# Two layers of cached attention and gated MLP on one core: weights through a ring of four equal places, block transposes between up and down, values that give up quarters

## The chip, the core and the metric

The kernel runs on one core of one Trainium2 chip. The time is device microseconds of one execution; smaller is better. Three runs of the kernel before took 2713.55, 2713.64 and 2716.07 us (median 2713.64 us). One further execution was profiled; it took 2714.15 us, of which 2712.4 us are the span from its first to its last instruction.

## What is computed

Two batch rows (B = 2) of width 576 pass twice through the same attention block and the same gated MLP:

```python
x = x + attention(layernorm(x))       # wq, K cache, V cache, wo
x = x + mlp(layernorm(x))             # (gelu(h @ w_gate) * (h @ w_up)) @ w_down
x = x + attention(layernorm(x))       # same weights, same caches
x = x + mlp(layernorm(x))
```

The caches hold 32 heads of 8192 positions by 128 floats for each batch row, in float32: one head of one batch row is 4.19 MB of keys and as much of values. The weights are wq 576x4096, wo 4096x576, w_gate and w_up 576x4608, and w_down 4608x576.

## The kernel before, in words

**Work.** There are 64 pairs of a head and a batch row, numbered n in the loop of `attention` (line 524). For each n the keys are multiplied by the query in four quarters (`multiply`, lines 401 to 417: VectorE multiplies 128x2048 elements, GpSimd adds the upper half of each head vector to the lower), `add_up` (line 419) reduces each quarter to scores on VectorE, `peak`, `highest` and `softmax` (lines 434 to 453) find the maximum and the exponentials through TensorE, VectorE and ScalarE, and `values` (line 463) multiplies them with the values: 16 matrix products on TensorE. The work of n-1 after its last quarter is interleaved by hand with the quarters of n (lines 524 to 553): this order is fixed in the program, engine by engine.

**Memory.** One tile `space` (line 102) of 50176 floats a partition holds all that is streamed in. It has five slots of 8192 floats, each for the keys or the values of one pair, and behind them, from RING = 40960 on, a sixth slot with 1024 floats more. In the MLP of layer 0 and at the start of attention 1 the weights pass only through the part behind RING, since the five slots before it hold what attention 1 will use first: the keys of the last two pairs and the values of the last three are kept from layer 0 (`keys_held`, `values_held`, line 223), and attention 1 walks the pairs backward (line 281).

**Order of the loads.** All loads are issued by the queue of SyncE, in one order: `plan_attention` and `plan_mlp` (lines 230 to 278) append them to a list, and `pump` (line 117) issues from its head as long as `Arena` finds free room; `done` (line 124) frees room and pumps again. A load waits for the last instruction that read or wrote what lay in its room, and everything behind it in the queue waits with it.

**Weights in layer 0's MLP.** w_gate and w_up come in nine pieces each of 2304 floats a partition (`ONE`, line 173); w_down comes in thirds of 1728 floats, the last of them split into 1152 and 576 (`thirds`, lines 217 to 219). Each is put where `Arena.ring` (line 74) finds room first. wq of attention 1 comes in nine pieces of 2048 floats, each to one of four fixed addresses (line 236).

**Start of attention 1.** The keys of pair 2 (counted in the backward walk) come in quarters to the room that wq left; those of pair 3 come in quarters to the room of pair 0's keys, those of pair 4 to that of pair 1's keys (line 245), each quarter as soon as `add_up` is done with the quarter that lay there. The values of pair 3 come next, whole, when all 16 products of `values(0)` are done (lines 477 to 481), then the keys of pair 5, whole, after `values(1)`.

**Between up and down.** `mlp` (line 575) scales the products of gate and up (`o`, lines 591 and 592), turns them to the layout that w_down needs by 18 small products on TensorE with a selection matrix `spread` (lines 595 to 601), copies the gate half out of PSUM, computes the GELU on VectorE and ScalarE (lines 605 to 610), writes `hT` (line 612) and multiplies with w_down (line 620).

Of the kernel before, what the change touches and what calls it, by code (L numbers as in the profile page):

```python
# [15 lines left out]
P = 128  # L16
# [15 lines left out]
EG = DF // 8  # L32
HG = EG // 2
# [7 lines left out]
END = NSLOT * SLOT + 1024  # L41
RING = 5 * SLOT
HELD = 5


class Arena:


    def __init__(self):
        self.live = {}  # L50
        self.freed = [0] * (NSLOT + 1)
        self.clock = 0
        self.at = RING

    def clear(self, lo, n):
        return all(hi <= lo or l >= lo + n for l, hi in self.live.values())

    def slot(self, key, allowed):

        for s in sorted(allowed, key=lambda s: self.freed[s]):  # L60
            if self.clear(s * SLOT, SLOT):
                for k in range(4):
                    self.quarter(key, s * SLOT, k)
                return s * SLOT
        return None

    def quarter(self, key, at, k):
        lo = at + k * PART
        if not self.clear(lo, PART):
            return False  # L70
        self.live[key, k] = (lo, lo + PART)
        return True
# [18 lines left out]
def decode_layers(ctx, tc, x_in, kc, vc, wq, wo, wg, wu, wd, out):  # L91
# [23 lines left out]
    queue, ready, slots = [], {}, {}  # L115

    def pump():
        while queue:
            t = queue[0][1]()
            if t is None:  # L120
                return
            ready[queue.pop(0)[0]] = t
# [5 lines left out]
    def cache(key, src, hb, allowed, pieces=1, where=None):  # L128

        rows = src[hb % B, hb // B].rearrange("(p j) d -> p j d", p=P)  # L130

        def load(at, lo, hi):
            t = space[:, at:at + SLOT].rearrange("p (j d) -> p j d", d=DH)
            nc.sync.dma_start(t[:, lo:hi, :], rows[:, lo:hi, :])
            return t

        def make():
            at = arena.slot(key, allowed)
            if at is None:
                return None  # L140
            slots[key] = at
            for lo in range(0, J, J // pieces):
                t = load(at, lo, lo + J // pieces)
            return t

        def make_quarter(k):
            at = slots[key] = RING if where == "ring" else slots[where]
            return load(at, k * JC, (k + 1) * JC) if arena.quarter(key, at, k) else None

        if where is None:  # L150
            queue.append((key, make))
        else:

            for k in ((NU + i) % 4 if where == "ring" else i for i in range(4)):
                queue.append((key, lambda k=k: make_quarter(k)))

    def eighths(key, w, us, width, lo, hi=None):

        n = 4 * len(us)

        def make():
            at = arena.ring(key, n * width, lo, hi)
            if at is None:
                return None
            t = space[:, at:at + n * width].rearrange("p (c w) -> p c w", c=n)
            src = w.rearrange("r (e w) -> (r e) w", w=width).rearrange("(p j) w -> p j w", p=P)
            nc.sync.dma_start(t, src[:, 4 * us[0]:4 * us[0] + n, :])
            return t

        queue.append((key, make))  # L170


    ONE = [range(u, u + 1) for u in range(NU)]
    THREE = [range(u, u + 3) for u in range(0, NU, 3)]
    PIECES = {
        ("wq", 0): THREE, ("wq", 1): ONE, ("g", 0): ONE, ("u", 0): ONE, ("g", 1): THREE, ("u", 1): THREE[:-1] + ONE[-3:],
    }

    def down(key, t0, lo, hi, first):

        def make():
            at = arena.ring(key, (hi - lo) * D, first)
            if at is None:
                return None
# [478 lines left out]
```

## Time and profile before

| what | value |
|---|---|
| median of the runs | 2713.64 us |
| profiled execution | 2714.15 us |
| its span | 2712.4 us |
| VectorE busy | 1887.3 us, 70% of the span |
| GpSimd busy | 1209.4 us, 45% |
| TensorE matmul busy | 1144.8 us, 42% |
| ScalarE busy | 82.6 us, 3% |
| packets of the SyncE queue, as a share of 16 DMA engines' span | 99.4% |

In the page the span is cut into 40 slices of 67.8 us; a digit is the busy share in tenths, and a row gives the GB/s in each slice. A row of a window table has the window, its length, the busy time of each engine with its instruction count, the granted TensorE clock, the mean busy share of the 16 DMA engines, and GB/s. A row of the chain of waits has the start, the length and the name of what the end waited for; "DMA tile<-source" there runs from a transfer's issue to its landing. A row of the timeline has start, length, engine, line, operation, tiles, shapes and count, and in brackets the idle time before it with what ended it; "SPq" is SyncE's queue issuing a transfer.

### The profile page before, as it was taken

What the parts mean: (1) busy time and instruction counts of PE and PEld (TensorE: products, weight loads), DVE (VectorE), ACT (ScalarE), POOL (GpSimd) and SP (SyncE); (2) the same over time, 40 slices, a digit from 0 to 9 for tenths busy, and PEclk for the clock granted to TensorE, in tenths of its full rate; (3) what the DMA queues carried; (4) which work ended last, traced back from release to release, by engine and by line L of the source; (5) the groups of instructions that cost most, each with busy time, mean ns of one, the idle gap of its engine ahead of it and who ended that gap; (6) DMA issues with size and microseconds to landing.
All of it is one profiled execution on the core that took longest, in us unless ns stands there. A gap on an engine that the chain in (4) does not pass through costs nothing.

```text
span 2712.4 us, 19378 instructions
## 1 busy us (share of the span) xinstructions
PE 1144.8 (42%) x7392; PEld 406.0 (15%) x7392; DVE 1887.3 (70%) x1809; ACT 82.6 (3%) x391; POOL 1209.4 (45%) x522
## 2 busy tenths in 40 slices
PE   2344434343434343444555434343434343434356
PEld 0111111111111111111211111111111111111122
DVE  5777777777777777776039877777777777777740
ACT  0000000000000000000000000000000000000000
POOL 3545454444445454443016554444444454445420
PEclk7666666666666666666757766666666666566667
DMA  9999999999999999999999999999999999999998
GB/s 418 432 433 431 431 430 431 432 432 431 430 432 432 431 431 431 431 432 414 404 358 409 430 431 432 432 431 430 431 431 432 431 430 431 432 431 431 432 426 378
DMA packets 49099, 1155.48 MB, mean 426 GB/s; under 512 B 5464, under 2 KB 5488, under 8 KB 7664
## 3 DMA queue, kind: packets, MB, share of 16 engines
q1 hardware_dynamic: 48968, 1154.24, 99.4%
q8 instruction: 58, 0.95, 0.1%
q14 instruction: 33, 0.27, 0.0%
q10 hardware_dynamic: 40, 0.01, 0.0%
HBM read 1154.23 MB, written 0.00 MB: 426 GB/s over the span
## 4 chain that ended last, share of the span: by engine, by line
DMA 80%; DVE 10%; PE 8%; issue 2%; POOL 0%; ACT 0%; DVEq 0%; POOLq 0%; SPq 0%; ACTq 0%
DMA space<-in_A_k_cache_dram 45%; DMA space<-in_A_v_cache_dram 28%; PE acc L472 7%; DVE space L413 5%; DVE S L422 3%; DMA space<-in_B_w_down_dram 2%; DMA space<-in_B_w_gate_dram 2%; DMA space<-in_A_wo_dram 1%; DMA space<-in_B_w_up_dram 1%; DMA space<-in_A_wq_dram 1%; DVE osb L489 1%; PE xps L620 0%; PE acc L584 0%; PE acc L377 0%; POOL space L417 0%
## 5 line engine op out<-in xcount | busy, mean ns | idle before, releaser
L417 POOL TENSOR_TENSOR space<-space 128x1024 f32<-128x1024 f32 x512 | 1206.4, 2356 | 1257.1 <-DVE space L413 1221.7
L413 DVE TENSOR_TENSOR space<-space,qp 128x2048 f32<-128x2048 f32 x512 | 1164.7, 2275 | 483.8 <-DMA space<-in_A_k_cache_dram 460.9
L472 PE MATMUL acc<-space,prz 128*8 128x512 f32 x4096 | 727.4, 874 | 290.1 <-DVE osb L489 170.6
L422 DVE TENSOR_REDUCE S<-space 128x16 f32<-128x1024 f32 x512 | 615.9, 1203 | 3.3 <-POOL space L417 3.3
L438 PE MATMUL mT<-ident,m 128*1 128x128 f32 x128 | 46.7, 365 | 794.2 <-DVE m L436 794.2
L472 PEld LDWEIGHTS acc<-space,prz 128*8 128x8 f32 x4096 | 133.7, 115 | 771.4 <-issue 723.5
L444 PE MATMUL nb<-m,ones 1*128 1x1 f32 x256 | 74.1, 356 | 254.8 <-DVE m L442 254.8
L438 PEld LDWEIGHTS mT<-ident,m 128*1 128x1 f32 x128 | 10.1, 79 | 820.0 <-DVE m L436 814.0
L457 PE MATMUL tot<-rs,ones 128*128 128x1 f32 x256 | 74.7, 361 | 92.7 <-ACT prz L451 92.7
L444 PEld LDWEIGHTS nb<-m,ones 1*128 1x128 f32 x256 | 63.1, 305 | 291.4 <-DVE m L442 291.4
L448 ACT ACTIVATE nbs<-nb 128x1 f32<-128x1 f32 x128 | 21.9, 171 | 2359.9 <-PE nb L444 2359.9
L503 DVE TENSOR_TENSOR oT<-po,rinv 32x16 f32<-32x16 f32 x64 | 10.9, 170 | 110.7 <-PE po L498 110.7
L363 POOL TENSOR_TENSOR rstd<-ve,mhalf 128x1 f32<-128x1 f32 x4 | 2.2, 552 | 174.0 <-DVE ve L361 174.0
L457 PEld LDWEIGHTS tot<-rs,ones 128*128 128x128 f32 x256 | 63.7, 309 | 104.0 <-ACT prz L451 103.5
L396 PE MATMUL qp<-qsb,pick 4*128 4x128 f32 x256 | 62.3, 325 | 27.9 <-DVE space L413 24.8
L584 PE MATMUL acc<-space,xt 128*8 128x288 f32 x576 | 56.3, 545 | 39.9 <-DMA space<-in_B_w_up_dram 19.9
L489 DVE SCALAR_TENSOR_TENSOR osb<-acc,diag,osb 128x128 f32<-128x128 f32 x192 | 67.3, 351 | 6.8
L592 DVE TENSOR_SCALAR o<-acc,rstd 128x288 f32<-128x288 f32 x2 | 1.0, 516 | 94.1 <-ACT o L591 94.1
L396 PEld LDWEIGHTS qp<-qsb,pick 4*128 4x128 f32 x256 | 38.0, 186 | 88.1 <-PE acc L472 48.5
L367 DVE TENSOR_TENSOR x<-xps,x 128x144 f32<-128x144 f32 x4 | 1.2, 308 | 70.8 <-PE xps L620 42.1
L498 PEld LDWEIGHTS po<-of,osb 128*32 128x32 f32 x512 | 40.1, 151 | 49.1 <-issue 39.6
L451 ACT ACTIVATE prz<-S,nbs 128x64 f32<-128x64 f32 x128 | 44.6, 348 | 4.4 <-ACT nbs L448 0.4
(56 smaller groups left out, 332.0 us busy)
## 6 DMA issues: line engine op xcount, KB each, us to landing
space<-in_A_k_cache_dram SPq DMA_DIRECT2D x123, 4096.0 KB
space<-in_A_v_cache_dram SPq DMA_DIRECT2D x123, 4096.0 KB
space<-in_A_wo_dram SPq DMA_DIRECT2D x16, 1152.0 KB
space<-in_B_w_up_dram SPq DMA_DIRECT2D x12, 1152.0 KB
space<-in_A_k_cache_dram SPq DMA_DIRECT2D x12, 1024.0 KB
space<-in_B_w_down_dram SPq DMA_DIRECT2D x13, 864.0 KB
space<-in_B_w_gate_dram SPq DMA_DIRECT2D x9, 1152.0 KB
space<-in_B_w_gate_dram SPq DMA_DIRECT2D x3, 3456.0 KB
```

The source lines that it names most:

```text
L396: nc.tensor.matmul(qb[n], pick[32 * c:32 * c + 4, r:r + 1].to_broadcast([4, P]), qsb[32 * c:32 * c + 4, (h % 4) * DH:(h % 4 + 1) * DH], st ...
L413: nc.vector.tensor_tensor(out=u, in0=t, in1=qb[n].unsqueeze(1).to_broadcast([P, JC, DH]), op=ALU.mult)
L417: nc.gpsimd.tensor_tensor(out=half, in0=half, in1=u[:, :, DH // 2:], op=ALU.add)
L422: nc.vector.tensor_reduce(out=S[n][:, k * JC:(k + 1) * JC], in_=prod.pop((n, k)), axis=AX.X, op=ALU.add)
L438: nc.tensor.transpose(mT[n], m, ident)
L444: nc.tensor.matmul(mT[n], ones[0:1, :], m1, start=True, stop=True)
L451: nc.scalar.activation(pr, S.pop(n).rearrange("p (g r) -> p g r", r=4), AF.Exp, bias=nbs, scale=scale, accum_out=rs[n],)
L457: nc.tensor.matmul(tot, ones, rs.pop(n), start=True, stop=True)
L472: nc.tensor.matmul(acc[32 * c:32 * c + 8, (n // B) % 2, :], prz[:, n % 3, at:at + 8], t[:, 4 * g:4 * g + 4, :].rearrange("p j d -> p (j d) ...
L489: nc.vector.scalar_tensor_tensor(t, q[:, r, :], diag[:, r:r + 1], t, op0=ALU.mult, op1=ALU.add,)
L498: nc.tensor.matmul(po[lo:lo + 32, i, :], t[:, i::GH], of, start=True, stop=True)
L584: nc.tensor.matmul(acc[32 * c:32 * c + 4 * B, s, :HG], xt[:, 32 * u + at:32 * u + at + 4 * B], w[:, 4 * (u - us[0]) + c, s * HG:(s + 1) * HG],
```

## The change

`Arena.ring` now hands out four places of 2304 floats each in turn; the weights of layer 0's MLP, the wo pieces of layer 0, the wq pieces of attention 1 and the key quarters of its pair 2 all take the next place (`first` is None). The search for room anywhere is kept under the name `fit`, for the first wq and for layer 1. w_down of layer 0 comes in eight pieces of four rows (2304 floats) and one that gathers the ninth row of all four blocks. In attention 1, `values` frees its room a quarter at a time; the values of pair 3 come in quarters to the room of pair 0's values, alternating with the key quarters of pair 4, and the keys of pair 5 come in quarters to the room of pair 1's values. For n = 1 of attention 1, `highest` and `softmax` of pair 0 stand ahead of the second `multiply`. In both MLPs the turn between up and down is made by two 32x32-block transposes of VectorE and four small copies, two on VectorE and two on ScalarE; the 18 products on TensorE and `spread` are gone. The matrix of ones is a broadcast of one column.

```diff
-EG = DF // 8
-HG = EG // 2
+HG = DF // 16
...
-END = NSLOT * SLOT + 1024
+PLACE = DF // 2
+NPLACE = 4
 RING = 5 * SLOT
+END = RING + NPLACE * PLACE
...
-    def ring(self, key, n, lo, hi=None):
+    def ring(self, key, n):
+
+        at = self.take(key, RING + self.turn % NPLACE * PLACE, n)
+        self.turn += at is not None
+        return at
+
+    def fit(self, key, n, lo=0):
 
         for at in [self.at, lo] + sorted(end for _, end in self.live.values()):
-            if lo <= at and at + n <= (hi or END) and self.clear(at, n):
-                self.live[key] = (at, at + n)
+            if lo <= at and at + n <= END and self.take(key, at, n) is not None:
                 self.at = at + n
                 return at
         return None
...
+    def cache_quarter(key, src, hb, k, where):
 
         def make():
-            at = arena.ring(key, n * width, lo, hi)
+            if where == "ring":
+                at = arena.ring((key, k), PART)
+            else:
+                at = arena.take((key, k), places[where][k], PART)
             if at is None:
-                return None
...
+                return False
+            cache_rows(at, hb, src, k * JC, (k + 1) * JC)
+            ready.setdefault(key, {})[k] = quarter(at)
+            return True
+
+        queue.append(make)
+
+    def weights(key, n, first, transfers):
 
         def make():
-            at = arena.ring(key, (hi - lo) * D, first)
+            at = arena.ring(key, n) if first is None else arena.fit(key, n, first)
...
+    DOWN = [
+        [[(t, i) for i in range(lo, lo + 4)] for t in range(NT) for lo in (0, 4)] + [[(t, NI - 1) for t in range(NT)]],
+        [[(t, i) for i in range(NI)] for t in range(NT - 1)]
+        + [[(NT - 1, i) for i in range(lo, hi)] for lo, hi in ((0, 3), (3, 6), (6, 8), (8, 9))],
+    ]
+
+    whole_at = (None, 0)
...
+            if layer and n == 4:
+                for turn, k in (("k", 0), ("v", 0), ("v", 1), ("k", 1), ("v", 2), ("v", 3), ("k", 2), ("k", 3)):
+                    if turn == "k":
+                        cache_quarter(key, kc, hb, k, ("k", 1, seq[1]))
+                    else:
+                        cache_quarter(("v", 1, seq[3]), vc, seq[3], k, ("v", 1, seq[0]))
+            elif layer and n in (2, 3, 5):
+                for k in range(4):
+                    cache_quarter(key, kc, hb, k, {2: "ring", 3: ("k", 1, seq[0]), 5: ("v", 1, seq[1])}[n])
...
-    ones = consts.tile([P, P], F32, name="ones")
-    nc.vector.memset(ones, 1.0)
+    one = consts.tile([P, 1], F32, name="one")
+    nc.vector.memset(one, 1.0)
+    ones = one.to_broadcast([P, P])
...
-            if not (held and layer == 0):
+                if left and g % 4 == 3:
+                    done((key, g // 4))
+            if left:
                 ready.pop(key)
-                for k in range(4):
-                    arena.free((key, k))
-                pump()
...
+            soon = layer == 1 and n == 1
+            if soon:
+                highest(n - 1)
+                softmax(n - 1)
             multiply(n, 1)
-            if before:
+            if before and not soon:
                 highest(n - 1)
                 softmax(n - 1)
...
-        gu = psum2.tile([P, NI, 2, NT * B], F32, name="gu", tag="small")
-        for i in range(NI):
-            for e in range(2):
-                nc.tensor.matmul(
-                    gu[64 * e:64 * e + 64, i, :, :], o[:, i::NI],
-                    spread[:, e, :, :, :].rearrange("p g t b -> p (g t b)"), start=True, stop=True,
-                )
...
-        nc.vector.tensor_copy(g, gu[:, :, 0, :])
...
+        turned = once.tile([P, NI, 32], F32, name="turned", tag="xc")
+        gu = once.tile([P, 2, 2, NI, 2 * B], F32, name="gu")
+        for v, to in enumerate((turned, o[:, 0, :].rearrange("p (i r) -> p i r", i=NI))):
+            nc.vector.transpose(to, o[:, v, :].rearrange("p (m i) -> p i m", i=NI))
+            for k in range(2):
+                (nc.vector.tensor_copy, nc.scalar.copy)[v](gu[:, k, v, :, :], to[:, :, 4 * k:4 * k + 4])
```

More of the change, by code (lines that the diff above doesn't have):

```diff
@@ L217, in decode_layers @@
[L217 to L220 removed]
+            at = [RING + k * PLACE for k in (2, 3)]
+            if not all(arena.clear(a, PLACE) for a in at):
+                return False
+            ready["products"] = [quarter(arena.take(("products", k), at[k], PART)) for k in range(2)]
+            return True
@@ L624, in mlp @@
+                        start=(rows is DOWN[layer][0] and k == 0), stop=(t, i) == (NT - 1, NI - 1),
                     )
-            done(("d", layer, t, lo, hi))
+            done(("d", layer, rows[0]))
         add_to_x()
```

233 lines of the change are left out of this document (101 added, 132 removed).

## The prediction

> **What bounds the kernel.** I read the page first, then a table of windows.
>
> ```profile
> span 2712.4 us, 19378 instructions
> GB/s 418 432 433 431 431 430 431 432 432 431 430 432 432 431 431 431 431 432 414 404 358 409 430 431 432 432 431 430 431 431 432 431 430 431 432 431 431 432 426 378
> L413 DVE TENSOR_TENSOR space<-space,qp 128x2048 f32<-128x2048 f32 x512 | 1164.7, 2275 | 483.8 <-DMA space<-in_A_k_cache_dram 460.9
> ...
> 60.00:1200.00 1140.00, 456.73 (x2508) 158.67 (x2500) 850.46 (x787) 35.50 (x174) 549.20 (x234) 0.64 1.00 431
> 1280.00:1300.00 20.00, 12.34 (x216) 5.87 (x208) 1.67 (x6) 0.00 (x0) 0.00 (x0) 0.75 0.91 362
> 1340.00:1360.00 20.00, 11.67 (x160) 5.87 (x164) 2.01 (x8) 0.77 (x2) 0.00 (x0) 0.67 0.85 336
> 1400.00:1420.00 20.00, 5.47 (x22) 1.53 (x14) 13.92 (x8) 0.69 (x1) 9.37 (x4) 0.50 0.84 329
> 1420.00:1440.00 20.00, 8.56 (x44) 3.33 (x44) 19.93 (x18) 1.22 (x6) 13.70 (x6) 0.67 0.89 334
> 2700.00:2713.00 13.00, 6.63 (x144) 4.46 (x144) 0.31 (x1) 0.00 (x0) 0.00 (x0) 0.87 0.40 163
> ```
>
> The loads set the time: 431 GB/s at a busy share of 1.00 for 1140 us on end, while VectorE, the busiest engine, waits 460.9 us for keys. No byte is taken away, so a gain can only come from stretches in which the stream runs thin: around 1290, 1350, 1410 and 1430 us, and the tail. The change touches the MLP of layer 0 (1300 to 1380) and the start of attention 1 (1400 to 1440). The second view is the chain of waits through both.
>
> ```profile
> 1339.83 8.93 DMA space<-in_B_w_up_dram
> ...
> 1348.80 2.18 PE acc L584 x16
> ...
> 1351.59 0.53 DVE o L592
> ...
> 1352.16 2.38 PE gu L598 x36
> ...
> 1356.59 3.10 PE xps L620 x48
> ...
> 1370.71 8.82 DMA space<-in_B_w_down_dram
> ...
> 1383.16 1.93 PE acc L377 x8
> 1385.11 6.88 DMA space<-in_A_wq_dram
> ...
> 1393.71 8.45 DMA space<-in_A_wq_dram
> ...
> 1405.81 2.30 DVE space L413
> ```
>
> The last piece of w_up lands at 1339.83 + 8.93 = 1348.76, the last of w_down at 1370.71 + 8.82 = 1379.53, the last of wq at 1393.71 + 8.45 = 1402.16; attention 1 starts on VectorE 3.65 later.
>
> **Part 1: the stall at w_down.** The timeline gives the pace of the stream and the issues.
>
> ```profile
> 1346.01 1.16 PE L584 MATMUL acc<-space,xt 128*8 128x288 f32 x16 [1.63 <-DMA space<-in_B_w_up_dram]
> 1348.80 2.11 PE L584 MATMUL acc<-space,xt 128*8 128x288 f32 x16 [1.64 <-DMA space<-in_B_w_up_dram]
> ...
> 1350.93 0.33 SPq L187 DMA_DIRECT2D space<-in_B_w_down_dram  x1
> ...
> 1357.31 0.33 SPq L187 DMA_DIRECT2D space<-in_B_w_down_dram  x1
> ...
> 1358.75 0.33 SPq L187 DMA_DIRECT2D space<-in_B_w_down_dram  x1
> ...
> 1356.59 6.30 PE L620 MATMUL xps<-space,hT 128*4 128x144 f32 x120 [2.07 <-DVE hT L612]
> ```
>
> Pieces of 2304 floats (1.18 MB) land 2.79 apart. w_down is nine such pieces, 25.1 us; it takes 1379.53 - 1348.76 = 30.8. So 5.7 us are lost, and the issues show where: four thirds are out by 1350.93, the fifth goes at 1357.31, after the first products with w_down. Four thirds are 4 x 2.09 = 8.4 us of stream: it is dry from 1357.1 on. In the changed program four pieces of 2304 lie in the same ring (its order of instructions shows each waiting for one piece of w_up), issued at the same moments, since they wait for the same products of L584: 11.2 us of stream, to 1359.9.
>
> The fifth piece then needs the chain up to `hT` and all 16 products of the first piece. The chain, from these rows:
>
> ```profile
> 1382.42 0.69 DVE L357 STREAM_TRANSPOSE xt<-xc 128x288 f32<-128x288 f32 x1
> ...
> 1354.57 0.23 DVE L605 COPY ga<-gu 128x72 f32<-128x72 f32 x1 [2.46 <-PE gu L598]
> ...
> 1355.60 0.26 ACT L609 ACTIVATE ga<-ga 128x72 f32<-128x72 f32 x1 [4.04 <-DVE ga L608]
> ```
>
> Out go 36 product records (2.38 from 1352.16) and the copy (0.23): the first arithmetic on g starts at 1354.83. In come, after `o` is done at 1352.12: two transposes of the very shape of L357 with its stride of nine (2 x 0.69), two VectorE copies of 36 elements between them (not in the trace; between 0 and the 0.23 of 72 elements: taken 0.15 each), one ScalarE copy of 36 elements (bounds 0 and the 0.26 of 72 elements; taken 0.2, near the upper since short work there hardly gets shorter) and about 0.1 for two handoffs. That is 2.0 us, start at 1354.1: 0.7 less, bounds 0.5 and 1.3. `hT` is then done at 1355.85 instead of 1356.55.
>
> The transfer issued at 1358.75 waited for the 16th product, 2.16 after the first. So the fifth piece goes out at 1355.9 + 2.15 = 1358.0. Into an empty queue a third landed within 4.4 us of its issue (the fifth third feeds the last 12 of the 60 products of the x120 row, which start about 1361.7), 2.3 above its 2.09 of stream; so this piece lands by 1358.0 + 2.79 + 2.3 = 1363.1, against 1359.9 + 2.79 = 1362.7 without a gap: 0.4 lost instead of 5.7. The gathered ninth piece has four runs of 2304 bytes a partition instead of one of 9216; no row has that, I add 0.2 (bounds 0, and 1.0 for a third slower). w_down lands 5.1 earlier. Without any gain in the chain it is 4.4; with all of it 5.5.
>
> What is late next is wq: its fifth piece (issued at 1385.11) needs the first wq product group, and that needs x. The last w_down piece now brings 16 products instead of four, so x is 1.5 later behind its landing: products of wq start 5.1 after it, the first group ends 1.9 after that, and the fifth piece lands 4.8 later (2.49 + 2.3), 11.8 behind the last w_down landing, where the stream has it at 5 x 2.49 = 12.5. It holds, with 0.7 to spare. So 5.1 us pass on to the start of attention 1.
>
> **Part 2: attention 1.**
>
> ```profile
> 1399.71 1.89 PE L377 MATMUL acc<-space,xt 128*4 128x512 f32 x8 [0.65 <-DMA space<-in_A_wq_dram]
> 1402.20 1.89 PE L377 MATMUL acc<-space,xt 128*4 128x512 f32 x8 [0.60 <-DMA space<-in_A_wq_dram]
> ...
> 1421.92 2.28 DVE L413 TENSOR_TENSOR space<-space,qp 128x2048 f32<-128x2048 f32 x1
> 1422.06 0.37 PE L438 MATMUL mT<-ident,m 128*1 128x128 f32 x1 [3.86 <-DVE m L436]
> 1424.12 0.27 DVE L442 TENSOR_REDUCE m<-mT 1x1 f32<-1x128 f32 x1
> 1426.28 5.39 PE L472 MATMUL acc<-space,prz 128*8 128x512 f32 x32
> ...
> 1425.54 0.33 SPq L134 DMA_DIRECT2D space<-in_A_k_cache_dram  x1
> ...
> 1435.58 0.33 SPq L134 DMA_DIRECT2D space<-in_A_k_cache_dram  x1
> ...
> 1462.38 0.33 SPq L134 DMA_DIRECT2D space<-in_A_k_cache_dram  x1
> ```
>
> I keep the clock of before; all of it moves with part 1. A quarter (1.05 MB) takes 2.49 in a full queue (the two wq landings, same size); whole keys take 4.19 MB / 431 = 9.73. VectorE frees key quarters only every 3.35 (1425.54 to 1435.58 in three steps), and the values of pair 3 stood behind them, though `values(0)` was done at 1431.7. The four quarters for pair 3 stay as they are.
>
> Moved: `highest` ahead of `multiply(1,1)`. VectorE now waits for the maximum's transpose (done 1422.43) and starts that multiply near 1422.77 instead of 1421.92; as L442 no longer follows it, the next `add_up` ends 0.64 later, and all behind it on VectorE too: the first key quarter of pair 4 goes at 1426.2. `values(0)` starts 1.65 earlier, 1424.6, and frees a quarter every 1.35, from 1426.0 on. So the first value quarters wait for nothing behind that key quarter, and eleven quarters (three of keys, four of values, four of pair 5's keys) follow without a gap: the last of them waits for the end of `values(1)`, one pair behind 1431.7: four steps of 3.35 and 0.64 later, 1445.7, before its turn. With the same landing time L in both: before, 1435.58 + L + 2 x 9.73 = 1455.0 + L; after, 1426.2 + L + 11 x 2.49 = 1453.6 + L. Gain 1.5, bounds 0.5 (quarters 0.09 slower each) and 2.1 (no delay on VectorE). Late next: pair 6's keys wait for `values(2)`, 1462.38 + 0.64 = 1463.0, and must go 2.3 and their own 9.73 before their turn to land, 9.73 behind the values ahead of them: at 1453.6 + 4.8 + 9.73 - 2.3 = 1465.8, where 4.8 is L (2.49 + 2.3): 2.8 to spare.
>
> The row that speaks against splitting would be a full-queue quarter far above 9.73 / 4 = 2.43; it is 2.49. The Trainium skill has a rule against it: its page DMA: Bandwidth & Descriptors, section "Anatomy of one DMA — SWDGE (gpsimd) path", gives each DMA a fixed 2.0 us besides its bytes. By that, an estimate from the page, six more transfers in a row would cost 12 us and the sum would turn to a loss of 5. The trace agrees with the rule for an empty queue (about 2.3) and not for a full one (2.49 against 2.43).
>
> **Costed at nothing.** First wq at other addresses: the second slice of the page already runs at 432 GB/s; if it did not, a late product group of wq would cost its 1.9. Broadcast ones: they feed products whose wait VectorE hides in its 460.9 us for keys, 3.7 a pair; without that cover, every 0.1 us would cost 12.8. Quarterwise release elsewhere: whole loads still wait for the 16th product. MLP of layer 1 saves 0.7 in a chain that no load waits for. Ring in turn for wo, gate and up: same order and the same products waited for, so the dip at 1280 stays.
>
> **Sum.** 5.1 + 1.5 = 6.6. The profiled execution has 2714.15 (span 2712.4): 2707.5, and its span 2705.8. The median is 0.5 below that execution: 2707.0.
>
> **Rivals.**
>
> ```profile
> 1358.00:1360.00 2.00, 2.00 (x40) 1.26 (x36) 0.00 (x0) 0.00 (x0) 0.00 (x0) 0.50 0.87 245
> 1360.00:1362.00 2.00, 2.00 (x48) 1.28 (x44) 0.00 (x0) 0.00 (x0) 0.00 (x0) 0.59 0.95 294
> 1362.00:1364.00 2.00, 0.89 (x32) 0.46 (x20) 0.00 (x0) 0.00 (x0) 0.00 (x0) 1.00 0.85 316
> ```
>
> (a) The slow restart comes back. After the gap 6 us ran at 245 to 316 GB/s with several thirds issued; against 1.18 MB / 2.79 = 423 that is 2.0 us lost. If this is no consequence of the gap, it returns: 2709.5. For it: busy shares of 0.85 to 0.95. Against: before the gap nothing ran so slowly.
> (b) The change doesn't do what it says, as the dips are none of the end's: the share is a mean over 16 engines, and the tail (163 GB/s) shows them ending apart; if one lags and catches up in every dip, little returns: 2712. Against: landings, which need the last engine, slip by 5.7.
> (c) Slower: the eleven quarters don't overlap. At 2.43 + 2.3 = 4.7 each they cost 11 x 2.24 = 24.6: 2731.6. It decides from 2.49 + 6.6 / 11 = 3.1 a quarter on. Against: the 2.49. The rule of the Trainium skill named above (DMA: Bandwidth & Descriptors, the same section) points this way.
> (d) More: the windows miss 9.2 us against 431 in 1400 to 1440; if half of that goes, 2704.
>
> **Chances.** Forecast 62% (own range 2705 to 2709), (a) 15%, (b) 10%, (c) 7%, (d) 6%. Faster by over 0.2% (5.4 us, about what can be told from no change here) means below 2708.2: nine tenths of the forecast and (d), 62%; within 31%; slower 7%. The range 2704 to 2711.6 leaves out (c) and some of (b) and (d).
>
> **What would show it.** Right: first product of w_down 0.5 to 1.3 sooner after L584 ends; w_down landing in 25 to 26 us; quarters 2.5 apart behind pair 4's first; keys of pair 6 issued before the stream is dry. Wrong: a window of 2 us near w_down below 200 GB/s; wq products waiting for room; TensorE's products of pair 0 no earlier.

## The result, and the profile after

| | before | after |
|---|---|---|
| median of 22 runs each, taken side by side | 2714.61 us | 2710.09 us |
| lowest and highest | 2711.72 to 2716.74 | 2708.31 to 2712.11 |
| ratio, 95% interval | | 0.9984 [0.9978, 0.9990] |
| the same in a second series (33 and 11 runs) | 2713.88 us | 2710.74 us, 0.9990 [0.9981, 0.9999] |
| profiled execution (its span) | 2714.15 (2712.4) | 2712.0 (2710.2) |

The change made the kernel 4.5 us faster in the first series and 3.1 in the second; about 4 is the best figure. Forecast were 6.6. Both medians lie in the stated range of 2704 to 2711.6, but above the forecast's own range of 2705 to 2709, by 1.1 and 1.7 us. The profiled execution of after is one of the slowest of its 22, so the two profiles lie only 2.15 apart; a second profile of the same kernel (below, 2710.64) is nearer to its median. Single executions of one kernel differ by 2 to 5 us here, so what follows never rests on one time alone.

The first view is the page of after, then the table of windows at the four places that the prediction named (columns as before: window, length, busy time of the engines, granted clock, DMA share, GB/s).

```profile
span 2710.2 us, 19231 instructions
...
GB/s 418 433 432 432 429 432 431 433 429 431 432 431 431 431 431 430 432 432 419 403 361 421 428 431 432 432 431 430 432 432 431 431 431 431 431 431 431 431 426 376
...
L425 DVE TENSOR_TENSOR space<-space,qp 128x2048 f32<-128x2048 f32 x512 | 1164.8, 2275 | 472.6 <-DMA space<-in_A_k_cache_dram 450.2
```

```profile
1280.00:1300.00 20.00, 11.41 (x208) 6.03 (x207) 1.58 (x5) 0.00 (x0) 0.00 (x0) 0.79 0.94 379
1340.00:1360.00 20.00, 10.07 (x132) 3.76 (x132) 3.27 (x11) 1.11 (x4) 0.00 (x0) 0.66 0.97 399
1400.00:1420.00 20.00, 4.50 (x18) 1.53 (x14) 14.89 (x9) 0.69 (x1) 9.64 (x5) 0.50 0.85 322
1420.00:1440.00 20.00, 9.53 (x48) 3.57 (x52) 19.46 (x17) 1.22 (x6) 13.78 (x6) 0.59 0.92 368
```

VectorE still waits 450.2 us for keys (460.9 before), and the full slices are as full as before. The stretch from 1340 to 1360 went from 336 to 399 GB/s and 1420 to 1440 from 334 to 368: the two places that the change aimed at. 1400 to 1420 stays thin. The chain of waits through the same part (start, length, what the end waited for):

```profile
1340.09 9.43 DMA space<-in_B_w_up_dram
...
1349.57 2.15 PE acc L604 x16
...
1352.86 0.61 DVE turned L617
...
1353.49 0.29 DVE gu L619 x2
1353.78 0.61 DVE o L617
...
1354.46 0.23 ACT gu L619
...
1356.48 2.14 PE xps L638 x32
1358.64 7.07 DMA space<-in_B_w_down_dram
...
1367.06 10.12 DMA space<-in_B_w_down_dram
...
1382.74 1.93 PE acc L390 x8
1384.69 4.95 DMA space<-in_A_wq_dram
...
1390.78 10.40 DMA space<-in_A_wq_dram
...
1404.84 2.30 DVE space L425
```

It is read as in the prediction. The last w_up piece lands at 1340.09 + 9.43 = 1349.52; the last w_down piece at 1367.06 + 10.12 = 1377.18, 27.7 later instead of 30.8; the last wq piece at 1390.78 + 10.40 = 1401.18, 24.0 after that instead of 22.6. The transposes and copies are the four rows from 1352.86 on. The fifth w_down piece, issued at 1358.64, takes 7.07 to land.

To weigh whole stretches I turn GB/s into lost time: length x (1 - GB/s / 431). So 30 us at 384 GB/s lose 3.3 us. The rows of before (from 1350 on) and then of after for this:

```profile
1350.00:1380.00 30.00, 20.17 (x332) 10.79 (x324) 2.01 (x8) 0.77 (x2) 0.00 (x0) 0.58 0.89 348
1380.00:1402.00 22.00, 14.22 (x66) 1.32 (x66) 2.41 (x8) 0.00 (x0) 0.55 (x1) 0.63 1.00 403
1402.00:1425.00 23.00, 4.80 (x17) 2.11 (x17) 18.89 (x13) 0.69 (x1) 12.44 (x6) 0.50 0.84 323
1425.00:1460.00 35.00, 18.03 (x97) 5.73 (x100) 34.82 (x31) 1.83 (x9) 22.83 (x10) 0.70 0.94 383
```

```profile
1270.00:1300.00 30.00, 18.94 (x304) 10.13 (x307) 3.51 (x12) 0.61 (x3) 0.00 (x0) 0.80 0.97 394
1300.00:1325.00 25.00, 15.65 (x158) 4.56 (x150) 2.42 (x8) 0.00 (x0) 0.55 (x1) 0.69 0.97 390
...
1350.00:1380.00 30.00, 16.14 (x304) 8.56 (x296) 3.83 (x13) 1.11 (x4) 0.00 (x0) 0.67 0.97 384
1380.00:1402.00 22.00, 13.72 (x70) 2.01 (x74) 1.86 (x7) 0.00 (x0) 0.55 (x1) 0.66 0.99 393
1402.00:1425.00 23.00, 5.90 (x27) 2.77 (x23) 19.39 (x13) 1.30 (x4) 12.66 (x6) 0.50 0.84 315
1425.00:1460.00 35.00, 18.24 (x94) 5.25 (x90) 34.82 (x32) 1.22 (x6) 22.77 (x11) 0.60 0.98 406
```

The same table for every kernel of the study, in us lost (between 1325 and 1350 all lose about 0.5), beside the time of that profiled execution, the median of the timed runs, and the ratio to the kernel before measured alongside:

| kernel | 1270 to 1325: wo, gate | 1350 to 1402: w_down, wq | 1402 to 1460: attention 1 | profiled run | median | ratio, 95% |
|---|---|---|---|---|---|---|
| before | 4.0 | 7.2 | 9.7 | 2714.15 | 2714.61 | 1 |
| after | 5.0 | 5.2 | 8.2 | 2712.0 | 2710.09 | 0.9984 [0.9978, 0.9990] |
| after, again | 4.8 | 4.6 | 7.5 | 2710.64 | 2710.74 | 0.9990 [0.9981, 0.9999] |
| turn on TensorE | 4.1 | 5.8 | 7.5 | 2710.81 | 2712.06 | 0.9990 [0.9981, 0.9999] |
| values whole | 4.9 | 5.3 | 9.4 | 2713.39 | 2712.22 | 0.9989 [0.9981, 0.9998] |
| thirds | 5.0 | 5.7 | 7.8 | 2712.78 | 2714.32 | 0.9999 [0.9990, 1.0008] |
| thirds, again | 5.0 | 7.7 | 7.1 | 2714.54 | 2713.27 | 0.9998 [0.9989, 1.0007] |
| all three undone | 4.7 | 7.3 | 10.2 | 2716.93 | 2716.59 | 1.0007 [0.9998, 1.0016] |
| small last piece | 4.9 | 5.7 | 7.9 | 2712.73 | 2710.53 | 0.9988 [0.9979, 0.9997] |
| half pieces | 4.3 | 3.8 | 6.6 | 2708.88 | 2709.03 | 0.9983 [0.9974, 0.9991] |
| early GELU | 5.1 | 2.7 | 6.2 | 2708.12 | 2709.70 | 0.9983 [0.9974, 0.9992] |
| short chain | 5.0 | 3.0 | 7.1 | 2708.88 | 2708.74 | 0.9982 [0.9973, 0.9991] |
| short chain, half pieces | 4.7 | 2.1 | 7.1 | 2708.34 | 2708.38 | 0.9979 [0.9971, 0.9988] |
| the same, gate in halves | 4.8 | 2.9 | 7.9 | 2709.83 | 2708.34 | 0.9977 [0.9969, 0.9986] |

A row's sum follows the time of its own profiled run to within 1.5 us: from before to early GELU it falls by 6.9 and the run by 6.0, from before to all three undone it grows by 1.3 and the run by 2.8. With before as the reference the others' runs are always a little longer than their rows say, by 0.2 to 1.5. The medians come from five series, in which the kernel before had 2713.9 to 2714.6, so that across series the ratios are the fairer figure. The medians of eleven runs have intervals of about 2.4 us to either side, so that differences between neighbours in this table are read together with the profiles, not alone.

### The profile page after: what moved, and what is told of

It reads as the page before. It is cut to its first block, busy times and chain, and to the rows that moved or that the text cites. A ratio compares the mean times of both kernels' runs of the same rounds, so it can differ in the third digit from the quotient of the medians.

```text
span 2710.2 us, 19231 instructions
## 1 busy us (share of the span) xinstructions
PE 1155.1 (43%) x7320; PEld 404.2 (15%) x7320; DVE 1888.4 (70%) x1799; ACT 83.2 (3%) x395; POOL 1208.4 (45%) x522
## 4 chain that ended last, share of the span: by engine, by line
DMA 77%; DVE 12%; PE 8%; issue 2%; POOL 0%; another core or an unknown queue 0%; ACT 0%; POOLq 0%; ACTq 0%; SPq 0%; DVEq 0%
DMA space<-in_A_k_cache_dram 44%; DMA space<-in_A_v_cache_dram 25%; PE acc L485 7%; DVE space L425 7%; DVE S L434 3%; DMA space<-in_B_w_down_dram 2%; DMA space<-in_A_wo_dram 2%; DMA space<-in_B_w_gate_dram 2%; DMA space<-in_B_w_up_dram 1%; DMA space<-in_A_wq_dram 1%; DVE osb L501 1%; PE xps L638 0%; POOL space L429 0%; PE acc L604 0%; PE acc L390 0%
## 5 line engine op out<-in xcount | busy, mean ns | idle before, releaser
L425 DVE TENSOR_TENSOR space<-space,qp 128x2048 f32<-128x2048 f32 x512 | 1164.8, 2275 | 472.6 <-DMA space<-in_A_k_cache_dram 450.2
L485 PE MATMUL acc<-space,prz 128*8 128x512 f32 x4096 | 742.3, 890 | 287.0 <-DVE osb L501 167.6
L456 PE MATMUL nb<-m,one 1*128 1x1 f32 x256 | 74.0, 356 | 252.7 <-DVE m L454 252.7
L450 PEld LDWEIGHTS mT<-ident,m 128*1 128x1 f32 x128 | 10.2, 79 | 805.8 <-DVE m L448 799.9
L469 PE MATMUL tot<-rs,one 128*128 128x1 f32 x256 | 74.5, 360 | 93.1 <-ACT prz L463 93.1
L456 PEld LDWEIGHTS nb<-m,one 1*128 1x128 f32 x256 | 63.1, 304 | 289.7 <-DVE m L454 289.7
L469 PEld LDWEIGHTS tot<-rs,one 128*128 128x128 f32 x256 | 63.6, 308 | 104.3 <-ACT prz L463 103.8
```

Of the source, the lines that this page charges most:

```text
L425: nc.vector.tensor_tensor(out=u, in0=t, in1=qb[n].unsqueeze(1).to_broadcast([P, JC, DH]), op=ALU.mult)
L450: nc.tensor.transpose(mT[n], m, ident)
L456: nc.tensor.matmul(mT[n], ones[0:1, :], m1, start=True, stop=True)
L469: nc.tensor.matmul(tot, ones, rs.pop(n), start=True, stop=True)
L485: nc.tensor.matmul(acc[32 * c:32 * c + 8, (n // B) % 2, :], prz[:, n % 3, at:at + 8], t[g // 4][:, g % 4 * 4:g % 4 * 4 + 4, :].rearrange(" ...
```

## The experiments

**Each part undone by itself.** Turn on TensorE:

```diff
...
-            nc.vector.transpose(to, o[:, v, :].rearrange("p (m i) -> p i m", i=NI))
-            for k in range(2):
-                (nc.vector.tensor_copy, nc.scalar.copy)[v](gu[:, k, v, :, :], to[:, :, 4 * k:4 * k + 4])
...
+        for i in range(NI):
+            for e in range(2):
+                nc.tensor.matmul(
+                    gu[64 * e:64 * e + 64, i, :, :], o[:, i::NI],
+                    spread[:, e, :, :, :].rearrange("p g t b -> p (g t b)"), start=True, stop=True,
+                )
...
```

The rest of this edit brings back `spread` and the layout of `hT` that these products need.

> The changed kernel with the turn between up and down made by the 36 small products of TensorE again, in both layers; all loads are the same. Both theories agree on the chain: from the last product with w_up to the first with w_down 5.7 us instead of 4.8. Theory (the fifth piece of w_down sets the loads from there): w_down lands 0.9 later, in about 28.5 us instead of 27.64, and the end is 0.9 later, about 2711.0. Rival (the transfers after the stall are paced by something else, so that the chain is no longer what they wait for): w_down lands in 27.6 as in the changed kernel, the end within 0.3 of it.

The timeline of this kernel has the chain of before again:

```profile
1348.87 1.16 PE L611 MATMUL acc<-space,xt 128*8 128x288 f32 x16 [1.63 <-DMA space<-in_B_w_up_dram]
...
1351.26 2.35 PE L625 MATMUL gu<-spread,o 128*64 128x16 f32 x36 [1.23 <-DVE o L619]
...
1355.68 6.70 PE L646 MATMUL xps<-space,hT 128*4 128x144 f32 x128 [2.07 <-DVE hT L638]
```

From the last w_up product (1348.87 + 1.16) to the first of w_down are 5.65 us, 0.85 more than after's 4.80 (1356.48 - 1351.68). But here those 16 products took 1.16 us, and in the profile of after 2.11: TensorE's granted clock alternates, and which phase falls on the products behind the last landing decides 0.95 us by chance (the two profiles of one kernel, thirds below, have 1.16 and 2.11 as well). So both profiles issue the fifth piece about 9.1 behind the last w_up landing, and w_down takes 27.7 us in both. The median is 2.0 above after's 2710.1, more than the 0.9 expected, but the ratio, 0.9990, is that of after in its second series, and the intervals overlap. The chain's size is shown by the timeline, its effect on the end is not shown by the times.

Values whole:

```diff
-            if layer and n == 4:
-                for turn, k in (("k", 0), ("v", 0), ("v", 1), ("k", 1), ("v", 2), ("v", 3), ("k", 2), ("k", 3)):
...
-            elif layer and n in (2, 3, 5):
+            if layer and n in (2, 3, 4):
...
-            if not (layer == 1 and (held or n == 3)):
+            if not (layer == 1 and held):
...
-            soon = layer == 1 and n == 1
+            soon = False
```

> The changed kernel with the second part undone: the values of pair 3 and the keys of pair 5 in attention 1 come whole again, the maximum of pair 0 stands behind the second multiply again. Theory (the eleven quarters without a gap are worth what the profiles show): the keys of pair 5 land 1.7 later against the last wq landing, the end is 1.5 to 1.7 later, about 2711.7. Rival (a mean over engines that end apart: the gain was none of the end's): within 0.4 of the changed kernel.

Its loss in attention 1 is 9.4 us, before has 9.7 and all three undone 10.2; the six kernels that have the quarters and no other new edit past 1402 and finish w_down near after's time (after twice, turn on TensorE, thirds twice, small last piece) have 7.1 to 8.2, 7.7 in the mean. Against the mean of the three with whole values, 9.8, that is 2.1 for the second part. The landings say the same. The trace records 16 landings for each of these transfers, as many as there are DMA engines (they are the updates of the transfer's semaphore); the last landing of pair 5's keys comes 57.6, 58.4 and 58.4 us behind the last of wq in before, values whole and all three undone, and 55.3 to 57.2, 56.0 in the mean, in the eleven profiles with quarters. The theory holds, a little above its range. The median is 2.1 above after's, but by the ratios (0.9989 against 0.9984 and 0.9990, the intervals overlap) the times alone would not show it.

Thirds:

```diff
-        [[(t, i) for i in range(lo, lo + 4)] for t in range(NT) for lo in (0, 4)] + [[(t, NI - 1) for t in range(NT)]],
+        [[(t, i) for i in range(lo, lo + 3)] for t in range(NT) for lo in (0, 3, 6)][:-1] + [[(NT - 1, 6), (NT - 1, 7)], [(NT - 1, 8)]],
```

> The changed kernel with w_down of layer 0 in thirds of 1728 floats again, the last one split into 1152 and 576; chain, attention and everything else as changed. By the forecast the larger pieces were worth 4.4 us: the end would be 4.4 later, 2714.5. Theory from the two profiles: w_down lands in 29.9 us instead of 27.64, but the last piece brings one product group instead of four, x is ready 1.5 sooner, wq's fifth and sixth pieces are issued sooner and wq lands in 22.6 us instead of 24.0: 2.3 lost, 1.4 won, the end 0.9 later, 2711.0.

> The version with w_down in thirds once more, since its median stood 4.3 above the changed kernel and its profile, the fastest of its eleven runs, only 0.8. If its first profile was a fast one and the forecast is right for the pieces (4.4 us): the median stays at 1.000 of the kernel before, 2714, w_down takes 30 us or more with the short chain. If the pieces are worth what the first profiles show (0.9 to 1.5): ratio about 0.9990, 2711.5, w_down in 28.8 to 29.5.

The medians are 4.2 and 3.2 above after's (2.2 to 4.1 us by the ratios), nearer to the forecast's 4.4 than to the theory's 0.9; w_down takes 28.8 us in the first profile and 29.9 in the second. The second profile shows one reason why the theory was too low:

```profile
1376.58 11.57 SPq L188 DMA_DIRECT2D space<-in_A_wq_dram  x6
```

In the ring taken in turn the last two thirds' pieces (1152 and 576 floats) hold a whole place of 2304 each, so the first wq piece is issued at 1376.58, 2.5 before the last w_down landing at 1379.08; before packed the pieces closely and issued it at 1374.02, 5.5 ahead of 1379.53. The first wq piece lands 3.53 behind the last of w_down and the second 3.22 behind the first, instead of 2.49 each. So the undone version loses what the pieces lose and something more that before did not have; the pieces by themselves are worth less than 3.2 to 4.2. The exact share is not settled.

**What stays when all three are undone.** The edit is the three diffs above together.

> The changed kernel with all three parts undone together: products of TensorE for the turn, w_down of layer 0 in thirds, the values of pair 3 and the keys of pair 5 whole with the maximum of pair 0 in its old place. What stays of the change are the edits costed at nothing: the ring taken in turn, the broadcast ones, the first wq at other addresses, release by quarters. By the forecast these are worth nothing and the time is that of the kernel before, within 1 us (ratio 1.000). Rival: each part alone undone cost 2.0, 2.2 and 4.3 us by the medians, 8.5 together against 4.1 for the whole change; if the parts add up, the edits costed at nothing cost 4.4 and this kernel is at 1.0016, 2718.5.

The ratio 1.0007 [0.9998, 1.0016] lies between the two expectations; its interval just includes the kernel before, and its upper end is the rival's 1.0016. Its wq takes 23.9 us against before's 22.6, with the first piece again late (issued 1376.06, last w_down landing 1379.83): that is 1.2 of the 2.1 us, and it comes with thirds in places, which the changed kernel does not have. The 0.9 that is left for the broadcast ones, the ring in turn and the release by quarters is within the interval. That the parts do not add up to the whole (2.0 + 2.1 + 4.2 by the medians, against about 4) is partly this and partly the spread of medians.

**A shorter chain.** Early GELU takes the gate half out of the chain:

```diff
             for us in GU[layer][g]:
...
+            turn(g)
...
-                                start=(g == 0 and u == 0), stop=(g == 1 and u == NU - 1),
+                                start=(u == 0), stop=(u == NU - 1),
```

Here `turn(0)` scales, turns and copies the gate half and computes its GELU into `a`; `turn(1)` scales and turns the up half and multiplies it in.

> The changed kernel with the gate half turned and its GELU computed while w_up still streams; after the last product with w_up only the up half is scaled, turned and multiplied in. The whole result is still computed. The chain up to the first product with w_down falls from 4.8 to about 3.4 us, the fifth piece of w_down goes out 1.35 sooner, about 1357.3, 3.4 before the four pieces ahead of it have landed. Theory 1 (the slow landing after the stall is the price of the queue having run dry): there is no dry stretch now, the piece lands at its turn, w_down lands in 25.1 to 25.7 us instead of 27.64, and the end is about 2.0 sooner, 2708. Theory 2 (a queue with one or two pieces in it is slow at each boundary, dry or not): the piece again takes 7 us from its issue, w_down lands in 26.3, and the end is 1.3 sooner or less.

From the last w_up product (1350.06 + 2.11) to the first of w_down (1355.53) are 3.4 us; w_down takes 25.9 and wq 22.6 us. The fifth piece still takes 6.26 from issue to landing, but is at its turn, as theory 1 has it. The profiled run is the fastest of its eleven; the median is 0.4 below after's first and 1.0 below its second, less than the 2.0 expected.

> The changed kernel itself once more, for a second profile and for times beside the next three. If its first profile is typical: w_down in 26.8 to 27.7 us, wq in 23.5 to 24.4, the last keys of pair 5 land 55.4 to 55.9 behind the last wq piece, end near 2710. If its first profile caught a late one (2712.0 against a median of 2710.1): w_up lands 0.5 to 1 sooner and the rest is the same.

Neither came out as written. w_up lands at 1349.44, no sooner than in the first profile, and w_down takes 27.9 us as there; wq takes 22.6 instead of 24.0, and that, with 0.7 us less lost in attention 1, is the difference between the two profiles. For wq the granted clock explains it at least in part: the 16 products behind the last w_down landing took 1.16 us here and 2.10 in the first profile, and the fifth wq piece went out 6.6 behind that landing instead of 7.5.

> The changed kernel with the gathered ninth piece of w_down split: three rows of 576 floats, and one by itself at the end, so that four products instead of 16 stand behind the last landing and x is ready 0.9 to 1.6 us sooner. Theory (the late x is what wq loses by: its fifth piece goes out too late): wq lands in 22.6 us instead of 24.0, the end is 1.4 sooner than the changed kernel, 2708.5. Rival (wq is slow after w_down whenever w_down had a dry stretch before it, as in the version with thirds, whose x was as early and whose wq took 23.9): wq stays at 23.5 to 24.4 and the end within 0.4 of the changed kernel.

```diff
-        [[(t, i) for i in range(lo, lo + 4)] for t in range(NT) for lo in (0, 4)] + [[(t, NI - 1) for t in range(NT)]],
+        [[(t, i) for i in range(lo, lo + 4)] for t in range(NT) for lo in (0, 4)] + [[(t, NI - 1) for t in range(NT - 1)], [(NT - 1, NI - 1)]],
```

A miss: the median is 0.2 below that of after taken alongside, and wq takes 24.4 us in the profile. In the second profile of after, with the late x, it took 22.6. Its fifth wq piece went out 6.8 behind the last w_down landing, hardly later than the 6.6 there. So what wq loses after such a w_down changes from run to run by more than this edit moves it, and why it lost 2.0 here stays open.

> Early GELU and the small last piece together, and the two copies between transposes and product given to the other engine each, so that none waits for a handoff at the end. From the last product with w_up to the first with w_down 3.2 us instead of 4.8. Theory 1 (dry stretch and late x are the whole loss): w_down in 25.1 to 25.9, wq in 22.6, the end 3.0 sooner than the changed kernel, 2707. Theory 2 (the median of the version with the early GELU did not fall, so the stream pays the same somewhere else): w_down and wq together stay above 50 us, the end within 0.7 of the changed kernel.

The edit is early GELU, the small last piece, and `(nc.scalar.copy, nc.vector.tensor_copy)[v]` for the two copies. The chain is 3.3 us, w_down 25.7, wq 22.6: theory 1 in the profile. The median is 2.0 below after alongside, where theory 1 had 3.0 and theory 2 less than 0.7.

> The changed kernel with w_down of layer 0 in 18 pieces of two rows (1152 floats) that take eight half places in turn; the chain is that of the changed kernel. The first room is free after 8 products instead of 16, so the ninth piece goes out 0.6 to 1.0 sooner (8.1 behind w_up's landing instead of 9.1), before the queue is dry at 11.2. Theory 1 (a dry queue costs): w_down in 25.5 to 26.3 us instead of 27.64, x 0.6 to 1.0 sooner, end 1.5 to 2.5 sooner. Theory 2 (each boundary between transfers costs in a thin queue): twice the boundaries, w_down in 28 us or more, end no sooner than the changed kernel.

```diff
-        at = self.take(key, RING + self.turn % NPLACE * PLACE, n)
-        self.turn += at is not None
+        size = 1 if n <= PLACE // 2 else 2
+        self.turn += self.turn % size
+        at = self.take(key, RING + self.turn % (2 * NPLACE) * (PLACE // 2), n)
+        self.turn += size * (at is not None)
...
-        [[(t, i) for i in range(lo, lo + 4)] for t in range(NT) for lo in (0, 4)] + [[(t, NI - 1) for t in range(NT)]],
+        [[(t, lo), (t, lo + 1)] for t in range(NT) for lo in (0, 2, 4, 6)] + [[(t, NI - 1), (t + 1, NI - 1)] for t in (0, 2)],
```

Twice the transfers, the same chain, and the median 1.7 us below after alongside. w_down takes 26.9 us, between theory 1 (to 26.3) and theory 2 (from 28). More boundaries did not make it slower, and the first room, handed on 8.1 instead of 9.1 behind w_up's last landing, made it shorter: this rules theory 2 out as the main cause.

> Early GELU with w_down in half pieces, the last two of one row each: the shortest chain and the earliest free room together. Counting from w_up's last landing the first freed room is issued about 6.6 us behind it instead of 9.1, 4.5 before the four places' 11.2 us of stream have landed. Theory (what w_down loses is about 4.5 us minus that lead, whether or not the queue runs dry; wq the same with 9.96 us of stream): both lose next to nothing, w_down in 25.1 to 25.6, wq in 22.5, and the end 0.5 below the version with the short chain alone: 2708.3. Rival (only a dry stretch costs): w_down as in the two versions before it, 25.7 to 26.9, the end as theirs.

The edit is that of the short chain with these half pieces, the last two of one row each. Where after's stream falls, this one's does not. One microsecond at a time, after and then this kernel:

```profile
1357.00:1358.00 1.00, 1.00 (x24) 0.63 (x20) 0.00 (x0) 0.00 (x0) 0.00 (x0) 0.50 1.04 433
1358.00:1359.00 1.00, 1.00 (x24) 0.62 (x20) 0.00 (x0) 0.00 (x0) 0.00 (x0) 0.50 0.47 194
1359.00:1360.00 1.00, 1.00 (x28) 0.62 (x20) 0.00 (x0) 0.00 (x0) 0.00 (x0) 0.57 0.75 157
1360.00:1361.00 1.00, 1.00 (x41) 0.80 (x36) 0.00 (x0) 0.00 (x0) 0.00 (x0) 1.00 0.69 203
1361.00:1362.00 1.00, 1.00 (x40) 0.71 (x32) 0.00 (x0) 0.00 (x0) 0.00 (x0) 1.00 0.93 387
1362.00:1364.00 2.00, 0.21 (x8) 0.00 (x0) 0.00 (x0) 0.00 (x0) 0.00 (x0) 1.00 0.98 327
```

```profile
1357.00:1358.00 1.00, 1.00 (x25) 0.60 (x18) 0.00 (x0) 0.00 (x0) 0.00 (x0) 0.50 1.03 415
1358.00:1359.00 1.00, 1.00 (x24) 0.63 (x20) 0.00 (x0) 0.00 (x0) 0.00 (x0) 0.50 1.00 401
1359.00:1360.00 1.00, 1.00 (x28) 0.67 (x24) 0.00 (x0) 0.00 (x0) 0.00 (x0) 0.64 1.05 424
1360.00:1361.00 1.00, 1.00 (x36) 0.57 (x28) 0.00 (x0) 0.00 (x0) 0.00 (x0) 1.00 1.02 410
```

The median is 2708.38, ratio 0.9979 [0.9971, 0.9988]: by its median below both kernels, by about 2 us below after (the intervals overlap). w_down takes 25.9 us, of which the half pieces' own pace (1.43 apart, twice that is 2.86 against 2.79) takes 0.6; so the expected 25.1 to 25.6 was too low by about that, and wq, in 22.4, loses nothing: the theory.

> The version before (early GELU, half pieces of w_down) with w_gate of layer 0 in 18 half pieces too, so that the first room after x is handed on after 8 products instead of 16. Between 1300 and 1320 us the changed kernel moved 380 GB/s against 431, 2.4 us lost. Theory (lead): room there 0.6 to 1.0 sooner, 1.4 to 1.8 us lost, the end 0.6 to 1.0 sooner than without: 2707.5. Rival (more transfers cost in a full queue): the end later.

`w_gate` of layer 0 comes in pieces `rows[:, u, v, :]` of 1152 floats, freed after the eight products of each half. Nothing came of it: 2708.34 against 2708.38. The window 1300 to 1325 went from 394 to 402 GB/s, and the one before it from 395 to 386.

## Why the prediction was right, and where it was off

**Direction and place: right.** The end moved with the loads, at the two places named, and the versions with thirds and with whole values lose again, in their profiles, at the place of their part; with the turn on TensorE the chain is longer, but w_down is not. By the times alone only the thirds (just) and all three undone stand clear of after's first series. That the median lies in the stated range is partly luck: the first part brought less than half of its 5.1 us, the second 0.6 more than its 1.5, and the range was drawn wide enough to hold rivals.

**The chain: right.** 5.68 us became 4.80, 0.88 against the 0.7 forecast, within the bounds of 0.5 and 1.3. On the chain each transpose takes 0.61, VectorE's two copies 0.29, and ScalarE's 0.23; taken were 0.69, 0.3 and 0.2.

**Attention 1: right, a little small.** `values(0)` starts 18.82 behind VectorE's start instead of 20.47 (1423.66 - 1404.84; before 1426.28 - 1405.81):

```profile
1404.84 4.49 DVE L425 TENSOR_TENSOR space<-space,qp 128x2048 f32<-128x2048 f32 x2 [22.16 <-PE qp L409]
...
1423.66 5.80 PE L485 MATMUL acc<-space,prz 128*8 128x512 f32 x32
...
1431.85 14.55 SPq L136 DMA_DIRECT2D space<-in_A_k_cache_dram  x6
...
1462.99 0.33 SPq L136 DMA_DIRECT2D space<-in_A_k_cache_dram  x1
```

That is the 1.65 of the forecast. The eleven quarters run without a gap (1425 to 1460 moved 406 and, in the second profile, 424 GB/s; before 383), and their landings are 2.49 apart. The keys of pair 6 go out at 1462.99. The forecast had 1463.0 on the clock of before, 60.8 behind the last wq landing; here it is 61.8, in the second profile 60.2, so the agreement of the two times is by chance. The part is worth about 2.1, by the lost time and by the landings (values whole, above), against 1.5 with an upper bound of 2.1.

**The step that failed: "this piece lands by 1363.1 against 1362.7 without a gap: 0.4 lost instead of 5.7".** The fifth piece went out 9.11 behind the last w_up landing, as reckoned (9.24), and its last landing came at 1365.71 instead of 1363.1. w_down lost 2.5 in one profile and 2.8 in the other, against 9 x 2.79 = 25.1. I had taken the stream to be dry only 11.2 behind the last landing, 1360.7 here, and a restart to cost 2.3. The windows show the stream at 194 GB/s from 1358 on, two microseconds earlier. The profile of before shows the same: its four thirds last to 1357.1 by that reckoning, and the stream has nearly stopped before that:

```profile
1354.00:1356.00 2.00, 0.52 (x10) 0.41 (x8) 1.00 (x5) 0.26 (x1) 0.00 (x0) 0.50 0.57 235
1356.00:1358.00 2.00, 1.42 (x27) 0.87 (x31) 0.50 (x3) 0.00 (x0) 0.00 (x0) 0.50 0.02 7
```

The landings show why. TensorE waits for the last of the 16 landings of a piece (those of w_up's last piece come from 1347.49 to 1349.53, its products start at 1349.57), and for the w_down pieces ahead of the gap these lie 1.6 to 3.0 us apart, by kernel. Those of the fourth piece of after come from 1358.61 to 1360.62, ten of the 16 by 1359.14. So most of the stream had run out by then, and the cover of four pieces is about 2 us shorter than counted from last landings. The restart itself was reckoned nearly right: the first landing of the fifth piece comes at 1363.43, 4.8 behind its issue, which is 2.0 above the 2.79 (1.9 to 2.0 in six further profiles with whole pieces), and 14 of the 16 are there by 1363.80.

The other kernels bear it out. Let the lead be 11.16 (8.36 with four thirds) minus the time from w_up's last landing to the issue into the first freed room, and the loss w_down's length above 25.1:

| kernel | lead | loss | sum |
|---|---|---|---|
| before | -0.2 | 5.7 | 5.5 |
| thirds; again | 0.7; -0.3 | 3.7; 4.8 | 4.4; 4.5 |
| after; again | 2.1; 2.1 | 2.5; 2.8 | 4.6; 4.9 |
| turn on TensorE | 2.1 | 2.6 | 4.7 |
| small last piece | 2.1 | 2.4 | 4.5 |
| values whole | 3.0 | 1.7 | 4.7 |
| all three undone | -0.2 | 5.0 | 4.8 |
| early GELU; short chain | 3.5; 3.6 | 0.8; 0.6 | 4.3; 4.2 |

The versions with half pieces stand apart, since their own pace takes 0.6. All but before lie at 4.2 to 4.9: every microsecond of lead below about 4.5 is lost, one for one. I had reckoned with 2.3, the restart alone. The 4.5 is about the restart of 1.9 to 2.0 and the spread of the fourth piece's landings, 2.0 to 3.0, together: 4.0 to 4.9 in the seven profiles with whole pieces. When the fifth piece has landed does not tell the loss: with the turn on TensorE its 16 landings came within 0.5 us, the last of them 5.15 behind the issue, as forecast (5.1), and w_down still lost 2.6, because the last landings of the four pieces behind it took 13.5 us instead of 11.2, while the landings drew apart again. Why they do so stays open.

Rival (a) had this size (2.0 us back, 2709.5) and is nearest to the medians of 2710.1 and 2710.7; its wording, a slow restart that is no consequence of the gap, is not what happened, since with enough lead (short chain and half pieces together) no window between 1356 and 1366 falls below 399 GB/s. Rival (b), a small return because the dips are a mean over engines that end apart, had the right observation: the landings of a piece do lie apart, and behind the gap the late ones had caught up (in before from 2.1 apart to 0.6). But little returned for another reason than it gives: the stream runs thin sooner than the last landing says. The tail bears the observation out too: the 16 landings of the last piece lie 6.7 us apart in before and 6.9 in after, more than the whole change brought, and nothing here touches that. Rivals (c) and (d) did not happen: the quarters overlap, and 1400 to 1440 still misses 8.0 us (322 and 368 GB/s) where it missed 9.2.

**"It holds, with 0.7 to spare" for wq: failed too.** By that row's reckoning after had a lead of 9.96 - 7.5 = 2.5 us in the first profile, where wq lost 1.6, and 9.96 - 6.6 = 3.4 in the second, where it lost 0.2. That the loss has the same cause is argued, not shown: the small last piece had 3.2 and lost 2.0.

**What was costed at nothing** lost up to 1 us: 1270 to 1325 loses 4.0 in the one profile of before and 4.1 to 5.1 in all kernels with the ring in turn. With one profile of before this may be chance.

The sum by what was measured: 7.2 - 4.9 = 2.3 for w_down and wq (4.9 is the mean of after's two profiles) instead of 5.1, 2.1 for attention 1 instead of 1.5, less up to 0.9 at wo and gate: 3.5 to 4.4, against 4.5 and 3.1 by the medians.

## What to carry to other kernels

Count the cover of a stalled stream from the window in which its mean rate falls, not from the last landing that an engine waits for: here that differed by 2 us, and a freed room had to be handed on about 4.5 us before the landings said it was needed. When the room cannot grow, shorten what stands between the last load and the first freed room: work that needs only the first half of the data can be done while the second half streams in, and the first room can be made smaller. A ring of equal places can cost when small pieces come last, since each holds a whole place: here the next weights then went out 2.5 us before the last landing instead of 5.5.

## What the runs showed of the hardware that was not expected

The same 16 products behind the last w_up landing took 1.16 us in some executions and 2.11 in others, with the granted clock between 0.50 and 1.00 from one microsecond to the next (the windows above): 0.95 us on the critical chain by chance, more than the edit to that chain was worth. Quarters and half pieces behind a full queue cost little more than their bytes: quarters land 2.49 apart, half pieces 1.43, against 2.79 for whole pieces. The Trainium skill (DMA: Bandwidth & Descriptors, section "Anatomy of one DMA — SWDGE (gpsimd) path") gives each DMA a fixed 2.0 us besides its bytes, for DMAs that GpSimd issues; the loads here are issued by SyncE. Into a drained queue the trace agrees (1.9 to 2.0, above). For transfers that wait in a full queue it does not: a half piece lands 1.43 us behind the one before it, less than the fixed part alone, and nine transfers more did not make the kernel slower.
